# The later modulation vectors: from 64 small matmuls on TensorE to 24 products on VectorE

## The chip, the cores and the metric

The kernel runs on one core of one Trainium2 chip. The metric is the time of one execution on the device in microseconds (us), the median of several executions. Before the change it is 836.27 us (three runs, 836.22 to 836.33), so differences of half a microsecond can be read if a kernel like it is run a few times.

Names used below: TensorE (PE in the profile) multiplies matrices, VectorE (DVE) and ScalarE (ACT) do elementwise work, GpSimd (POOL) and SyncE (SP) mostly issue DMA here. HBM is the memory of the chip, SBUF the on-chip memory, of which the kernel uses 128 partitions.

## The reference

A transformer block on 2048 tokens of 1024 values, with six modulation vectors that come from one vector `c`:

```python
mod = (silu(c) @ w_mod).reshape(c.shape[0], 6, 1, -1)   # w_mod is 1024 x 6144
sa, ca, ga, sb, cb, gb = ...                            # six vectors of 1024
h = layernorm(x) * (1 + ca) + sa
x = x + ga * attention(h, wqkv, wo)     # linear attention: phi(q) (phi(k)^T v), 32 heads
h = layernorm(x) * (1 + cb) + sb
x = x + gb * (silu(h @ w_gate) * (h @ w_up)) @ w_down
```

All of it is in two-byte floats. `sa` and `ca` are needed at once. `ga`, `sb` and `cb` are the later vectors that the change is about: `ga` is needed as a row on all partitions (it multiplies the columns of `wo`), `sb` and `cb` as columns (one value per partition, for each of the 8 groups of 128 features).

## The kernel before

The tokens are handled in four chunks (`sc`). For each chunk TensorE makes the keys, the values and, before the next chunk's keys go on, the product of the last chunk's keys and values (`kv_phase`): 128 matmuls of 32x64. The later vectors are made between key groups:

```python
    def mod_rows(blks):                       # four 512-column blocks of w_mod at once
        ps = acc_b("modr")
        for j in range(DC):
            for g in range(4):
                mm(ps[32 * g:32 * g + 32, :], lhsT=sc32[:, j, :], rhs=blks[g][:, j, :],
                                 start=(j == 0), stop=(j == DC - 1))
        row = small.tile([P, NB], BF16, name="mrow", bufs=1)
        nc.scalar.copy(out=row[:], in_=ps[:])
        return row

    def mod_spread(k, row):                   # rows to HBM, and back as columns
        for g in range(4):
            nc.gpsimd.dma_start(out=mrow_dram[k, g:g + 1, :], in_=row[32 * g:32 * g + 1, :])
        cols = small.tile([P, 2 * DC], BF16, name="mcol", bufs=1)
        ...
            nc.gpsimd.dma_start(out=cols[:], in_=mrow_dram[1].rearrange("g (i p) -> p (g i)", p=P))
        nc.vector.tensor_copy(out=sbT[:], in_=cols[:, 0:DC])
        ...
    # ga_rows: the same for ga with 32 matmuls of 256 columns; its row goes to HBM
    # in four stores of 512 bytes and comes back on all partitions

    for sc in range(NSC):
        if sc > 0:
            k_phase(sc, 0, 2)
            kv_phase(sc - 1)
            k_phase(sc, 2, 4)
            if sc == 2:
                ga_rows(blks)
            if sc == 3:
                mod_spread(1, mod_rows(blks))
            k_phase(sc, 4, 8)
            ...
        v_phase(sc)
        ...
```

## Time and profile before

| | before |
|---|---|
| median time | 836.27 us |
| span of the profiled execution | 834.7 us |
| TensorE busy | 828.2 us, 99% |
| VectorE busy | 317.6 us, 38% |
| modulation matmuls of the later vectors | 0.99 + 1.84 us |

The page of the profile of before, part 1 (busy time of each engine, with the share of the span and the number of instructions), and the head of part 4 (the chain of work that ended last, by engine):

```profile
span 834.7 us, 11272 instructions
...
PE 828.2 (99%) x4641; PEld 378.6 (45%) x4641; DVE 317.6 (38%) x606; ACT 168.6 (20%) x253; POOL 67.5 (8%) x168
...
PE 95%; DMA 3%; SPq 1%; DVE 0%; issue 0%; ACT 0%
```

TensorE is busy for all but 6.5 us, and the chain is TensorE, save for loads in the start-up and 2.9 us of ScalarE and VectorE at 168.5 us. So a microsecond of TensorE work that is taken out anywhere after the start-up is a microsecond of time, as long as nothing makes TensorE wait in its place.

The chain of before around the two places (start, length, link of the chain, number of instructions):

```profile
95.55 0.99 PE modr L98 x32
...
120.82 1.15 PE kvp L98 x128
121.97 3.56 PE acc L98 x16
125.53 1.84 PE modr L98 x32
```

`modr` are the modulation matmuls; both are links, so 0.99 + 1.84 = 2.83 us is what their removal can bring.

### The profile page before, as it was taken

Reading aid. Unit: us, or ns where it says so; the run is one execution under the profiler, and the core shown is the slowest. Engines: PE = TensorE matmul, PEld = TensorE weight load, DVE = VectorE, ACT = ScalarE, POOL = GpSimd, SP = SyncE. Lnnn points to the kernel's source line nnn. Section 1 sums busy time; section 2 is a strip of 40 time slices with the busy share of each in tenths; the row PEclk is TensorE's granted clock in tenths of the full one; section 3 lists DMA queues with packets and bytes.
Section 4 is the critical chain, followed back from the end, with each engine's and each line's share of the span. In section 5 each row is a group of like instructions: output and inputs, shape, how many; then the busy total and the mean of one; then the engine's idle time right before and its main releaser. Section 6 shows DMA issues by size and latency. Waiting matters only on the chain.

```text
span 834.7 us, 11272 instructions
## 1 busy us (share of the span) xinstructions
PE 828.2 (99%) x4641; PEld 378.6 (45%) x4641; DVE 317.6 (38%) x606; ACT 168.6 (20%) x253; POOL 67.5 (8%) x168
## 2 busy tenths in 40 slices
PE   8999999999999999999999999999999999999998
PEld 3444444444444444444444444444444444444444
DVE  5755643587344335522222244211114431111122
ACT  3455443334211111101111110111110101111000
POOL 2101201111130201100000010000001100000000
PEclk9999999999999999999999999999999999999999
DMA  9873790129998644636434183662505529710011
GB/s 325 293 202 88 227 194 1 34 61 290 359 247 265 190 151 144 185 117 219 144 114 138 44 227 95 220 221 82 171 1 155 162 69 332 239 53 1 19 58 51
DMA packets 125748, 129.07 MB, mean 155 GB/s; under 512 B 34112, under 2 KB 106304, under 8 KB 125184
## 3 DMA queue, kind: packets, MB, share of 16 engines
q1 hardware_dynamic: 121440, 114.97, 45.7%
q0 software_dynamic: 3968, 12.99, 5.4%
q8 instruction: 36, 0.59, 0.3%
q10 hardware_dynamic: 288, 0.40, 0.1%
q14 instruction: 16, 0.13, 0.1%
HBM read 108.27 MB, written 12.72 MB: 145 GB/s over the span
## 4 chain that ended last, share of the span: by engine, by line
PE 95%; DMA 3%; SPq 1%; DVE 0%; issue 0%; ACT 0%
PE acc L98 88%; PE a_ps L98 7%; DMA wv<-in_A_wqkv_dram 1%; DMA x_sb<-in_A_x_dram 1%; DMA wme<-in_w_mod_dram 1%; PE kvp L98 1%; SPq L140 0%; PE modr L98 0%; PE den L98 0%; SPq L120 0%; DVE wo L577 0%; PE wf L98 0%; SPq L137 0%; DVE pq L292 0%; ACT eb L289 0%
## 5 line engine op out<-in xcount | busy, mean ns | idle before, releaser
L98 PE MATMUL acc<-h2T,wgu 128*128 128x512 bf16 x1792 | 387.6, 379 | 0.0
L98 PEld LDWEIGHTS <-wgu 128*128 128x128 bf16 x1792 | 175.3, 98 | 211.3
L98 PE MATMUL acc<-wd,gu 128*128 128x512 bf16 (+2 forms) x924 | 196.1, 373 | 0.0
L646 DVE TENSOR_TENSOR gu<-acc,e 128x512 bf16<-128x512 f32 x112 | 77.5, 692 | 289.9 <-PE acc L98 289.9
L645 ACT ACTIVATE e<-acc 128x512 f32<-128x512 f32 x112 | 66.9, 597 | 374.8 <-PE acc L98 374.8
L98 PEld LDWEIGHTS <-gu 128*128 128x128 bf16 x924 | 89.3, 98 | 104.5
L98 PEld LDWEIGHTS <-hT 128*128 128x128 bf16 x512 | 49.6, 98 | 60.0 <-issue 1.4
L667 DVE TENSOR_TENSOR e<-acc,gb_bc 128x512 f32<-128x512 f32 (+2 forms) x33 | 22.3, 675 | 131.5 <-PE acc L98 128.6
L98 PE MATMUL a_ps<-wo,pq 128*128 128x512 bf16 x256 | 57.4, 379 | 0.0
L98 PE MATMUL acc<-wk,hT 128*128 128x512 bf16 x256 | 57.1, 379 | 0.0
L98 PE MATMUL acc<-hT,wq 128*128 128x512 bf16 x256 | 56.8, 379 | 0.0
L98 PE MATMUL acc<-wv,hT 128*128 128x512 bf16 x256 | 56.1, 379 | 0.3 <-DMA wv<-in_A_wqkv_dram 0.3
L289 ACT ACTIVATE eb<-acc 128x512 bf16<-128x512 f32 x64 | 37.8, 596 | 74.1 <-PE acc L98 71.0
L228 ACT ACTIVATE xn<-x,nmr,rstd 128x1024 bf16<-128x1024 f32 x16 | 19.8, 1240 | 126.2 <-POOL nmr L226 126.2
L614 POOL DMA_DIRECT2D x_scratch<-x x16 | 9.9, 616 | 377.3 <-DVE x L607 377.3
L98 PEld LDWEIGHTS <-pq 128*128 128x128 bf16 x256 | 25.1, 98 | 30.2
L98 PEld LDWEIGHTS <-wq 128*128 128x128 bf16 x256 | 24.6, 98 | 29.8 <-issue 0.9
L290 DVE TENSOR_SCALAR eb<-eb 128x512 bf16<-128x512 bf16 x64 | 18.5, 294 | 49.4 <-ACT eb L289 49.3
L607 DVE TENSOR_TENSOR x<-a_ps,x_sb 128x512 f32<-128x512 f32 x32 | 22.1, 691 | 7.8 <-PE a_ps L98 7.7
L212 POOL TENSOR_TENSOR rstd<-veps,neg_half 128x1 f32<-128x1 f32 x32 | 17.9, 560 | 80.9 <-DVE veps L210 70.8
L327 ACT CAST v<-acc 128x512 bf16<-128x512 f32 x32 | 18.2, 582 | 23.2 <-PE acc L98 23.2
L670 DVE TENSOR_TENSOR ob<-e,x1r 128x512 bf16<-128x512 f32 (+2 forms) x33 | 22.3, 676 | 1.0
(82 smaller groups left out, 274.6 us busy)
## 6 DMA issues: line engine op xcount, KB each, us to landing
wgu<-in_B_w_gate_dram SPq DMA_DIRECT2D x28, 1024.0 KB, 7.3
wgu<-in_B_w_up_dram SPq DMA_DIRECT2D x28, 1024.0 KB, 8.8
x_sb<-in_A_x_dram SPq DMA_DIRECT2D x32, 256.0 KB, 7.2
x_scratch<-x POOLq DMA_DIRECT2D x16, 512.0 KB, 3.1
x1r<-x_scratch SPq DMA_DIRECT2D x31, 256.0 KB, 2.8
wd<-in_B_w_down_dram SPq DMA_DIRECT2D x7, 1024.0 KB, 7.3
wml<-in_w_mod_dram SPq DMA_DIRECT2D x6, 1024.0 KB, 9.0
rbc<-rden_scratch POOLq DMA_DIRECT2D x16, 256.0 KB, 9.3
```

The lines of the kernel that those rows point to most:

```text
L98: return tc.keep_in_program_order(nc.tensor.matmul(out, lhsT=lhsT, rhs=rhs, start=start, stop=stop))
L212: nc.gpsimd.tensor_tensor(out=rstd[:, 0:n], in0=veps[:, 0:n], in1=neg_half[:].to_broadcast([P, n]), op=ALU.pow)
L228: nc.scalar.activation(out=dst, in_=src, func=ACT.Identity, bias=nmr[:], scale=rstd[:, 0:1])
L289: nc.scalar.activation(out=e[:], in_=acc, func=ACT.Exp)
L290: nc.vector.tensor_scalar(out=e[:], in0=e[:], scalar1=1.0, scalar2=PHI_EPS, op0=ALU.min, op1=ALU.add)
L327: nc.scalar.copy(out=v[:, t * D + nb * NB:t * D + (nb + 1) * NB], in_=acc[:])
L607: nc.vector.tensor_tensor(out=x1[:, ns], in0=a_ps[:], in1=x_t[:, ns], op=ALU.add)
L614: nc.gpsimd.dma_start(out=x1_dram[st * P:(st + 1) * P, :], in_=x1[:])
L645: nc.scalar.activation(out=sg[:], in_=ps[0][:], func=ACT.Silu)
L646: gm = nc.vector.tensor_tensor(out=guT[sc][f // GPT][:, f % GPT, :], in0=ps[1][:], in1=sg[:], op=ALU.mult)
L667: nc.vector.tensor_tensor(out=yt, in0=y_ps, in1=gb_bc[:, ns], op=ALU.mult)
L670: nc.vector.tensor_tensor(out=ob, in0=yt, in1=x1r, op=ALU.add)
```

## The change

The intent is to take the later vectors off TensorE. Blocks of `w_mod` are read by transposing loads, so that output features lie on partitions and inputs along the free axis. VectorE multiplies each 128x1024 block by silu(c), held as a row on all partitions, and sums along the row; the sum is one column of `ga`, `sb` or `cb`. There are 24 such products, set between VectorE's other work. `sb` and `cb` are wanted as columns, so their way through HBM goes away. `ga` is wanted as a row, so its column now has to be turned, by way of HBM. The loads of `wo` and its eight multiplications by `ga` move to the last chunk, and some orders of issue change; the cut below leaves that out.

```diff
-    def mod_rows(blks):
-        ps = acc_b("modr")
-        for j in range(DC):
-            for g in range(4):
-                mm(ps[32 * g:32 * g + 32, :], lhsT=sc32[:, j, :], rhs=blks[g][:, j, :],
-                                 start=(j == 0), stop=(j == DC - 1))
 ... (ga_rows, mod_load, mod_spread go as well)
+    def mod_load(q, cols):
+        for h in range(2):
+            t = big("wmt", [DC // 2, D])
+            lo = q * D + h * NB
+            last = nc.sync.dma_start_transpose(t[:], w_mod[:, lo:lo + NB])
+            mod_steps.extend((t[:, i, :], cols[:, 4 * h + i:4 * h + i + 1]) for i in range(DC // 2))
+        return last
+
+    def mod_step(n, anchor=None):
 ...
+                last = nc.vector.scalar_tensor_tensor(out=rows, in0=rows, scalar=scale, in1=sc_row[:], op0=ALU.mult,
+                                               op1=ALU.mult, accum_out=col)
+
+    def ga_spread():
+        col = small.tile([P, DC], BF16, name="gcol", bufs=1)
+        nc.vector.tensor_copy(out=col[:], in_=gaT[:])
+        with nc.allow_non_contiguous_dma(reason="1024 elements, once"):
+            nc.gpsimd.dma_start(out=ga_dram[0].rearrange("(i p) -> p i", p=P), in_=col[:])
+        nc.gpsimd.dma_start(out=ga_bc, in_=ga_dram[:].to_broadcast([P, D]))
 ... (start-up: sc_row is made by 8 small matmuls in place of some warming matmuls)
             kv_phase(sc - 1)
-            k_phase(sc, 2, 4)
-            if sc == 2:
-                ga_rows(blks)
-            if sc == 3:
-                mod_spread(1, mod_rows(blks))
-            k_phase(sc, 4, 8)
 ...
+            k_phase(sc, 2, 8)
 ...
+        if sc + 1 < NSC:
+            with tc.issue_after(last_load[0].ins):
+                last_load[0] = mod_load(*((2, gaT), (3, sbT), (4, cbT))[sc])
```

More of the change, by code (lines that the diff above doesn't have):

```diff
@@ L116 @@
     x_tiles = {}
+    last_load = [None]
     def load_x(st, eng):
         x_sb = k2.tile([P, D], BF16, name="x_sb")
-        eng.dma_start(out=x_sb[:], in_=x2[st * P:(st + 1) * P, :])
+        last_load[0] = eng.dma_start(out=x_sb[:], in_=x2[st * P:(st + 1) * P, :])
         x_tiles[st] = x_sb
@@ L187 @@
     sbT = const.tile([P, DC], F32, name="sbT")
+    cbT = const.tile([P, DC], F32, name="cbT")
     cb1T = const.tile([P, DC], F32, name="cb1T")
+    gaT = const.tile([P, DC], F32, name="gaT")
+    sc_row = const.tile([P, D], BF16, name="sc_row")
     ga_t = ep.tile([P, NB], F32, name="e")
@@ L206, in build_masks @@
                 nc.gpsimd.memset(zmask[rs, hg, HG * h + hg:HG * h + hg + 1], 1.0)
+    last_veps, last_nmr = [None], [None]
     def rstd_of(mv, n):
         veps = small.tile([P, STC], F32, name="veps")
-        nc.vector.tensor_scalar_add(out=veps[:, 0:n], in0=mv[:, 0:n, 1], scalar1=LN_EPS)
+        last_veps[0] = nc.vector.tensor_scalar_add(out=veps[:, 0:n], in0=mv[:, 0:n, 1], scalar1=LN_EPS)
         rstd = small.tile([P, STC], F32, name="rstd")
@@ L225, in normalise_act @@
         nmr = small.tile([P, 1], F32, name="nmr")
-        nc.gpsimd.tensor_scalar(out=nmr[:], in0=mv[:, 0, 0:1], scalar1=rstd[:, 0:1], scalar2=-1.0,
+        last_nmr[0] = nc.gpsimd.tensor_scalar(out=nmr[:], in0=mv[:, 0, 0:1], scalar1=rstd[:, 0:1], scalar2=-1.0,
                                 op0=ALU.mult, op1=ALU.mult)
@@ L255, in ln1_norm @@
         if sc > 0:
-            nc.sync.dma_start_transpose(hTs[sc][:, :, t * P:(t + 1) * P], xn[:])
+            last_load[0] = nc.sync.dma_start_transpose(hTs[sc][:, :, t * P:(t + 1) * P], xn[:])
         return xn
@@ L314, in k_phase @@
             k_evac(sc, [g], accs)
+            mod_step(int(k_groups.index(g) in K_STEPS[sc]))
     def v_phase(sc):
@@ L327, in v_phase, with q_phase @@
                 nc.scalar.copy(out=v[:, t * D + nb * NB:t * D + (nb + 1) * NB], in_=acc[:])
-    def q_phase(sc, lo=0, hi=DC):
+    def q_phase(sc, lo=0, hi=DC, steps=0):
         if lo == 0:
@@ L337, in q_phase @@
             phi_to(pqs[sc][:, qc, :], acc[:])
+            mod_step(steps)
     def v_ones(v, lo):
@@ L353, in kv_phase @@
         else:
-            nc.vector.tensor_tensor(out=kv_acc, in0=kv_acc, in1=kvv, op=ALU.add)
+            with tc.issue_after(last_phi[0].ins):
+                nc.vector.tensor_tensor(out=kv_acc, in0=kv_acc, in1=kvv, op=ALU.add)
     def gb_load():
@@ L368, in gb_sum @@
                 nc.vector.scalar_tensor_tensor(out=gb_acc[:], in0=t[:], scalar=sc, in1=gb_acc[:], op0=ALU.mult, op1=ALU.add)
-    def ga_rows(blks):
-        ps = acc_b("modr")
-        H2 = NB // 2
-        for j in range(DC):
-            for g in range(4):
-                mm(ps[32 * g:32 * g + 32, 0:H2], lhsT=sc32[:, j, :], rhs=blks[g // 2][:, j, (g % 2) * H2:(g % 2 + 1) * H2],
-                   start=(j == 0), stop=(j == DC - 1))
-        row = small.tile([P, NB], BF16, name="mrow", bufs=1)
-        nc.scalar.copy(out=row[:, 0:H2], in_=ps[:, 0:H2])
-        for g in range(4):
-            nc.gpsimd.dma_start(out=mrow_dram[0, g:g + 1, 0:H2], in_=row[32 * g:32 * g + 1, 0:H2])
-        nc.gpsimd.dma_start(out=ga_bc.rearrange("p (g n) -> p g n", g=4),
-                            in_=mrow_dram[0, :, 0:H2].unsqueeze(0).to_broadcast([P, 4, H2]))
@@ L384 @@
-    gb_rows = []
-    def mod_load(cols):
-        blks = []
-        for lo in cols:
-            t = big("wml", [DC, NB])
-            nc.sync.dma_start(out=t[:], in_=wm_v[:, :, lo:lo + NB])
-            blks.append(t)
-        return blks
-    def mod_rows(blks):
-        ps = acc_b("modr")
-        for j in range(DC):
-            for g in range(4):
-                mm(ps[32 * g:32 * g + 32, :], lhsT=sc32[:, j, :], rhs=blks[g][:, j, :],
-                                 start=(j == 0), stop=(j == DC - 1))
-        row = small.tile([P, NB], BF16, name="mrow", bufs=1)
-        nc.scalar.copy(out=row[:], in_=ps[:])
-        return row
@@ L404 @@
-    mrow_dram = dram.tile([2, 4, NB], BF16, name="mrow_scratch")
-    def mod_spread(k, row):
-        for g in range(4):
-            nc.gpsimd.dma_start(out=mrow_dram[k, g:g + 1, :], in_=row[32 * g:32 * g + 1, :])
-        cols = small.tile([P, 2 * DC], BF16, name="mcol", bufs=1)
-        with nc.allow_non_contiguous_dma(reason="2048 elements, once"):
-            nc.gpsimd.dma_start(out=cols[:], in_=mrow_dram[1].rearrange("g (i p) -> p (g i)", p=P))
-        nc.vector.tensor_copy(out=sbT[:], in_=cols[:, 0:DC])
-        nc.vector.tensor_scalar_add(out=cb1T[:], in0=cols[:, DC:2 * DC], scalar1=1.0)
+    gb_rows = []
@@ new lines @@
+    ga_dram = dram.tile([1, D], BF16, name="ga_scratch")
+    mod_steps = []
+    def mod_load(q, cols):
[6 more added lines that the diff above has]
+    def mod_step(n, anchor=None):
+        if n == 0:
+            return
+        scale = 1.0
+        if anchor:
+            one = small.tile([P, 1], F32, name="one", bufs=1)
+            with tc.issue_after(last_nmr[0].ins):
+                nc.gpsimd.memset(one[:], 1.0)
+            scale = one[:]
+        with tc.issue_after(anchor or last_phi[0].ins):
+            for _ in range(n):
+                rows, col = mod_steps.pop(0)
+                last = nc.vector.scalar_tensor_tensor(out=rows, in0=rows, scalar=scale, in1=sc_row[:], op0=ALU.mult,
+                                               op1=ALU.mult, accum_out=col)
+        return last
@@ L415, in modulate_all @@
+    K_STEPS = [(), (), (0, 2), (0, 2, 4, 5, 6)]
+    V_STEPS = [0, 4, 4, 7]
+    def ga_spread():
[4 more added lines that the diff above has]
+        nc.gpsimd.dma_start(out=ga_bc, in_=ga_dram[:].to_broadcast([P, D]))
     def modulate_all(hT, scaleT, biasT):
@@ L459, in keep_warm, with keep_warm_f32 @@
             mm(acc[:], lhsT=sel[:, 0, :], rhs=sel[:], start=True, stop=True)
+    def keep_warm_f32(acc, n):
+        zeros = sel[:].rearrange("p h n -> p (h n)").bitcast(F32)
+        for _ in range(n):
+            mm(acc[:, 0:zeros.shape[1]], lhsT=zeros[:, 0:P], rhs=zeros, start=True, stop=True)
     gs = k_groups[0:6]
@@ L463 @@
     spare = accs[5]
-    keep_warm(spare, 9)
+    keep_warm_f32(spare, 4)
+    keep_warm(spare, 1)
     hT = hTs[0] = big("hT", [DC, SCW])
@@ L477 @@
         xns = [ln1_norm(*st0)] + [ln1_norm(*ln1_stats(0, t)) for t in range(1, 3)]
-        keep_warm(spare, 6)
+        keep_warm_f32(spare, 3)
         mod_rows_a(0)
         pe_transpose_tile(hT, xns[0], 0)
-        keep_warm(spare, 3)
+        for h in range(2):
+            for j in range(DC // 2):
+                mm(accs[h][:, j * P:(j + 1) * P], lhsT=scT[:, 4 * h + j:4 * h + j + 1].to_broadcast([P, P]), rhs=ident[:],
+                   start=True, stop=True)
+            nc.scalar.copy(out=sc_row[:, h * NB:(h + 1) * NB], in_=accs[h][:])
         mod_rows_a(1)
@@ L521 @@
             kv_phase(sc - 1)
-            k_phase(sc, 2, 4)
-            if sc == 2:
-                ga_rows(blks)
-            if sc == 3:
-                mod_spread(1, mod_rows(blks))
-            k_phase(sc, 4, 8)
-            if sc == 1:
-                blks = mod_load([2 * D, 2 * D + NB])
-            if sc == 2:
-                blks = mod_load([3 * D, 3 * D + NB, 4 * D, 4 * D + NB])
+            if sc == NSC - 1:
+                wo = [big("wo", [4, D]) for _ in range(2)]
+                for h in range(2):
+                    for g in range(4):
+                        with tc.issue_after(last_load[0].ins):
+                            nc.sync.dma_start(out=wo[h][g * DH:(g + 1) * DH, :, :], in_=wo_v[h, g])
+            k_phase(sc, 2, 8)
         v_phase(sc)
@@ L537 @@
             q_phase(0, 0, 6)
+        steps = mod_step(V_STEPS[sc], last_veps[0].ins if sc + 1 < NSC else None)
+        if sc == NSC - 1:
+            with tc.issue_after(steps.ins):
+                for cc in range(DC):
+                    w = wo[cc // 4][:, cc % 4, :]
+                    nc.vector.tensor_tensor(out=w, in0=w, in1=ga_bc, op=ALU.mult)
+        if sc == 2:
+            with tc.issue_after(last_veps[0].ins):
+                ga_spread()
         if sc + 1 < NSC:
@@ L545 @@
                 load_x(st, nc.sync)
-        if sc == 2:
-            wo = [big("wo", [4, D]) for _ in range(2)]
-            for h in range(2):
-                for g in range(4):
-                    nc.sync.dma_start(out=wo[h][g * DH:(g + 1) * DH, :, :], in_=wo_v[h, g])
-            for cc in range(DC):
-                w = wo[cc // 4][:, cc % 4, :]
-                nc.vector.tensor_tensor(out=w, in0=w, in1=ga_bc, op=ALU.mult)
-    q_phase(1, 0, 2)
+        if sc + 1 < NSC:
+            with tc.issue_after(last_load[0].ins):
+                last_load[0] = mod_load(*((2, gaT), (3, sbT), (4, cbT))[sc])
+    q_phase(1, 0, 1, 2)
+    q_phase(1, 1, 2)
     kv_phase(NSC - 1)
@@ L682 @@
     q_phase(2, 6, 8)
+    nc.vector.tensor_scalar_add(out=cb1T[:], in0=cbT[:], scalar1=1.0)
     q_phase(3, 0, 5)
```

## The prediction

> # Prediction
>
> **What bounds the kernel now.** TensorE. The page gives it 828.2 us busy of a span of 834.7 us (99%) at full granted clock, and the chain of waits is 95% TensorE. After the start-up (it ends at 31.5 us with a load of the V weights) the waits view shows one TensorE wait, 0.2 us. VectorE is busy 317.6 us (38%), but nearly full in places: from 97.2 to 106.3 us its timeline idles 0.3 us.
>
> **What the change removes.** The late vectors (ga, sb, cb) cost 64 small matmuls: 0.99 us at 95.5 us and 1.84 us at 125.5 us, both links of the chain of waits, so all 2.83 us are critical. Off the path go two ScalarE evictions (0.37, 0.59 us), eight row stores, a column load, and a 2.23 us VectorE wait for it.
>
> **What it adds.** VectorE gets 24 products of 128x1024, each summed along the row. The nearest operation in the trace (scalar-tensor-tensor, 128x1024, gb sum) takes 1.28 us. Bf16 tensor-tensors of that size go at 0.62 us (four in 2.50)[...]; with reading out the sum I estimate a pitch of 1.2 to 1.3 us, 30 us in all. In the start-up, 8 small matmuls and two ScalarE copies replace three warming matmuls, where TensorE waits for loads: neutral. Six 1 MB loads become transposing loads. A 256 KB transpose takes 1.23 us of queue and lands in 3.5 us; I estimate 5 us of queue and 8 to 15 us to land. Each pair has 23 us or more before its first use: no wait.
>
> **Does VectorE delay TensorE?**
> - First stretch (from 78 us): VectorE idles 6.5 us there; four products fit, and TensorE needs the result only near 87 us.
> - Second (from 107 us): four products end near 112.5 us; TensorE needs the activations at 116 us.
> - Third, the tight place: between 127 and 153 us VectorE must do 12 products, the eight wo multiplies (4.9 us, moved here) and six activation pairs of 0.95 us, before the bf16 kv state that TensorE transposes near 153.4 us (156.2 now, less 2.8). My sum ends at 138.2 us + 12 pitches: 152.6 us for 1.2, 153.9 for 1.3, 155.1 for 1.4. So a stall of 0 to 2 us, most likely 0 to 0.5.
>
> After 175 us nothing changes but the start.
>
> **Predicted time: 833.7 us** (2.8 saved, about 0.3 given back), range 832.9 to 836.0. Chances: faster by over 2% 0.01, within 2% 0.98, slower by over 2% 0.01.
>
> **What would show each step right or wrong.**
> - TensorE busy falls by about 2.8 us; no modulation matmuls in the chain after the start-up.
> - The products show 1.2 to 1.3 us each; VectorE busy rises by about 30 us.[...]
> - The only new TensorE wait is at the transpose of the kv state, for VectorE, under 2 us.
> - The transposing loads land within 15 us; no product waits for one.
> - The start-up ends within 0.3 us of before.
>
> **What would make it wrong.** A transposing load out of HBM much slower than one out of SBUF (above 23 us for a pair), which would block VectorE and the evictions; a pitch of 1.5 us, which would eat the gain in the third stretch; fp32 warming matmuls that fail to hold the clock; loads that delay the transposes of the next activations.

With reading out the sum it came to the pitch of 1.2 to 1.3 us that stands in the text, which is 30 us for 24 products; the forecast's own sum, 138.2 us + 12 pitches, is built on it. The nearest operation in the trace of before, at 1.28 us, lies in the same range. As for the fear at the end that the clock might not hold: the granted clock in the start-up (0 to 32 us) was 1.00 in before, and 1.00 in after.

## More of the kernel before

Note for later how the vectors reach HBM before: TensorE makes them as rows, and each store writes 512 or 1024 bytes in one run.

The line that turns out to matter is the first DMA in `ga_spread`. `"(i p) -> p i"` lets partition p write value i to place 128 i + p of a row of 1024: by this pattern no value lies beside another of its partition, so the store is 1024 pieces of two bytes, and pieces of 32 partitions lie in each 64 bytes of HBM. Such a piece is called a write in what follows; the traces do not count them (the profile of e4 has 57 packets for this store).

`kvp` is the product of keys and values: 128 matmuls in 1.15 us.

## The result, and the profile after

| | before | after |
|---|---|---|
| median time | 836.3 us (836.22 to 836.33, 4 runs) | 847.62 us (846.95 to 849.78, 4 runs) |
| ratio after / before | | 1.014 (95% interval 1.0121 to 1.0159) |
| TensorE busy | 828.2 us | 824.4 us |
| VectorE busy | 317.6 us | 344.8 us |

Ratios here and below are the mean time of one kernel's fast runs over the mean of the other's in the same rounds, so they are not quite the ratio of the medians quoted. The change costs 11.3 us where 2.6 us of gain were predicted. It stays within 2%, but the time lies well outside the predicted range of 832.9 to 836.0.

The page after, the same lines:

```profile
span 846.2 us, 11100 instructions
...
PE 824.4 (97%) x4503; PEld 380.6 (45%) x4582; DVE 344.8 (41%) x654; ACT 168.7 (20%) x253; POOL 63.0 (7%) x162
...
PE 97%; issue 2%; DVE 1%; ACT 0%; POOL 0%
```

TensorE's work did shrink, but the chain now has 2% of "issue", time in which TensorE waited for nothing that the profile can name. The waits view of after (in total, times, longest) says where:

```profile
PE kvp L98 <- issue: 9.4, 4, 6.8
PE acc L98 <- issue: 2.2, 7, 1.0
```

Before has no such line. The wait for VectorE that the prediction looked for, at the transposes of the kv state, isn't there. The chain of after shows the place, the product of the third chunk's keys and values and the key groups behind it:

```profile
119.48 0.80 PE kvp L98 x86
120.28 0.49 issue
120.77 0.19 PE kvp L98
120.96 0.12 issue
121.08 0.27 PE kvp L98 x5
121.36 1.73 issue
123.08 0.21 PE kvp L98 x2
123.29 6.79 issue
130.09 0.38 PE kvp L98 x12
130.46 0.35 issue
130.81 0.52 PE kvp L98 x22
131.33 0.33 issue
131.66 1.91 PE acc L98 x4
133.57 1.05 issue
134.62 11.70 PE acc L98 x45
```

The product that took 1.15 us in before runs 86 matmuls at full speed and then trickles until 131.33 us. Four matmuls of the next key group follow, then one more stop. What was going on beside it? The windows view of after (busy us of each engine with instructions, then the granted TensorE clock, the DMA share, and GB/s moved):

```profile
115.00:117.00 2.00, 2.00 (x11) 0.93 (x10) 1.80 (x6) 0.59 (x1) 0.00 (x0) 1.00 1.25 276
119.00:121.00 2.00, 1.47 (x90) 0.77 (x87) 1.97 (x5) 0.60 (x1) 0.00 (x0) 1.00 1.94 35
125.00:127.00 2.00, 0.00 (x0) 0.00 (x0) 0.00 (x0) 0.00 (x0) 0.00 (x0) 0.50 1.87 18
131.00:133.00 2.00, 1.67 (x26) 0.75 (x19) 0.43 (x1) 0.00 (x0) 0.73 (x2) 0.50 1.54 174
```

From 119 to 131 us the DMA engines hold transfers all the time (the share, 1.50 to 2.16, is that of transfers in progress) and move 15 to 35 GB/s, against 276 before and 174 after. And TensorE, which stands still from 123.29 us, is granted half its clock (0.50) from about 125 us, so that it also works at half speed when it goes on: four matmuls take 1.91 us at 131.66, and 1.03 us in e1 below.

Two DMA issues frame the stretch. The timelines of GpSimd and of SyncE in after (start, length, queue, what is issued, how many; in brackets the idle time before):

```profile
113.30 1.13 POOL L415 DMA_DIRECT2D ga_scratch<-gcol  x1 [5.34 <-DVE gcol L413]
131.45 0.59 POOL L416 DMA_DIRECT2D e<-ga_scratch  x1 [17.02 <-PE kvp L98]
110.97 20.68 SPq L388 DMA_TRANSPOSE wmt<-in_w_mod_dram  x2
```

The dense store of the `ga` column is issued at 113.30, and the load that reads it back only at 131.45 (the profile of after names TensorE's product as what released it; in e2 and e3 below it names the landing of the store). The last pair of transposing loads is issued at 110.97, the second one blocks the queue of SyncE until 131.65. So there are two suspects, the store and the transposing loads, and both are new.

### The profile page after: what moved, and what is told of

Same layout as the page of the kernel before. It is cut to its first block, busy times and chain, and to the rows that moved or that the text cites. A ratio compares the mean times of both kernels' runs of the same rounds, so it can differ in the third digit from the quotient of the medians.

```text
span 846.2 us, 11100 instructions
## 1 busy us (share of the span) xinstructions
PE 824.4 (97%) x4503; PEld 380.6 (45%) x4582; DVE 344.8 (41%) x654; ACT 168.7 (20%) x253; POOL 63.0 (7%) x162
## 4 chain that ended last, share of the span: by engine, by line
PE 97%; issue 2%; DVE 1%; ACT 0%; POOL 0%
PE acc L98 89%; PE a_ps L98 6%; PE kvp L98 1%; DVE stats L224 0%; PE mod_ps L98 0%; PE den L98 0%; ACT xn L234 0%; DVE wo L592 0%; PE tp L101 0%; PE wf L98 0%; DVE pq L298 0%; ACT eb L295 0%; POOL rstd L218 0%; DVE mv L225 0%; DVE veps L216 0%
## 5 line engine op out<-in xcount | busy, mean ns | idle before, releaser
L98 PE MATMUL acc<-wk,hT 128*128 128x512 bf16 x251 | 59.0, 392 | 1.7 <-issue 1.5
L234 ACT ACTIVATE xn<-x,nmr,rstd 128x1024 bf16<-128x1024 f32 x16 | 19.8, 1240 | 126.0 <-POOL nmr L232 126.0
L623 DVE BATCH_NORM_STATS2 stats<-x 128x6 f32<-128x512 f32 x32 | 22.2, 694 | 1.1
```

The lines of the kernel that those rows point to most:

```text
L98: return tc.keep_in_program_order(nc.tensor.matmul(out, lhsT=lhsT, rhs=rhs, start=start, stop=stop))
L234: nc.scalar.activation(out=dst, in_=src, func=ACT.Identity, bias=nmr[:], scale=rstd[:, 0:1])
L623: nc.vector.bn_stats(out=stats[:, nb, :], in_=x1[:, ns])
```

## The experiments

### The theories

- **Store**: the dense store of 1024 two-byte values is slow in itself, holds the DMA engines and through them TensorE.
- **Transposing loads**: the last pair of transposing loads out of HBM holds the engines, and the store only waits behind it.

In the expectations of e1 to e4 these are theories A and C; theory B there is that the store does harm only beside the transposing loads. Later expectations use the letters anew, each time with its meaning.

All kernels below give right results within the tolerance, the first two only because the error that they make is small. Where a kernel was looked at once, its time has no interval, and the record gives its state as unknown, where it calls all the repeated runs fast; such runs are used for differences of several microseconds and for their traces.

### e1: the same store, but each partition writes its 8 values in one run (wrong: the row is permuted)

```diff
-            nc.gpsimd.dma_start(out=ga_dram[0].rearrange("(i p) -> p i", p=P), in_=col[:])
+            nc.gpsimd.dma_start(out=ga_dram[0].rearrange("(p i) -> p i", i=DC), in_=col[:])
```

> One edit to the changed kernel: the store of the ga vector to HBM writes each partition's 8 values (16 bytes) side by side instead of 1024 single values of 2 bytes; same bytes, same place, WRONG RESULT ON PURPOSE (ga comes back in another order). Theory A (the 1024 two-byte writes block the DMA engines' write path, and TensorE's next block of instructions waits behind it): the stop of TensorE in the kv product at 120 us goes, the last pair of transposing loads lands in about 7 us each, time 832.5 to 834.5. Theory B (the two-byte store is harmful only beside transposing loads): the same here. Theory C (transposing loads and instruction fetch collide, whatever the store): stays at 845 to 849.

Measured: 835.25 us (834.82 to 836.12), before 836.39; ratio 0.9985 (0.9968 to 1.0001). The chain of e1 at the same place:

```profile
120.39 1.16 PE kvp L98 x128
121.54 0.16 issue
121.70 1.03 PE acc L98 x4
122.73 1.82 issue
124.55 9.89 PE acc L98 x45
```

The stop in the product is gone, with the transposing loads unchanged. The time lies 0.75 us above theory A's range. Set against the chain of after this also splits the loss. From the start of the product to the end of the 45 matmuls after takes 134.62 + 11.70 - 119.48 = 26.84 us, e1 14.05 us. Of the 12.8 us between them, "issue" makes up 8.9 (10.86 against 1.98), and the same matmuls running slower, at half clock, 3.9 (15.98 against 12.07). One stop stays, of 1.82 us, after the 4th matmul of the key group; it comes back below.

### e2: the last pair as plain loads (wrong: `cb` is then not `cb`)

```diff
+            if q == 4:
+                last = nc.sync.dma_start(out=..., in_=wm_v[:, :, lo:lo + NB])
+            else:
                 last = nc.sync.dma_start_transpose(t[:], w_mod[:, lo:lo + NB])
```

> One edit to the changed kernel: the last pair of loads (for cb) is an ordinary load of the same bytes into the same tiles instead of a transposing one, WRONG RESULT ON PURPOSE; the two-byte store stays. Theory A: the store still needs more than 10 us to land, and TensorE still stops for several us in the kv product: 840 or more. Theory B: the store lands within about 5 us, no stop, 833 to 835. Theory C: no stop, 833 to 835.

Measured, one look: 848.96 us. TensorE stops in the same product (7.7 us of "issue" in all) and after the 4th matmul behind it (3.4 us). The transposing pair is not needed for the harm.

### e3: the dense store twice, to two places

> One edit to the changed kernel: the two-byte store is made twice, to two places in HBM. Theories A and B: the time in which the engines crawl (14 us, from 117 to 131 us) doubles to some 28 us and the stop of TensorE grows by 10 to 14 us: 857 to 863. Theory C: no change, 846 to 850. Result correct.

Measured, one look: 854.48 us, 6.9 us more than after. The stop in the product is 10.6 us at its longest, the one behind it 5.1 us. All the expected times were missed (857 to 863, 846 to 850). A second store adds about half of what the first one does; I put that down to two stores that are partly under way together, which no run separates.

### e4, e9, e10, e11: the store alone, in a quiet stretch of the kernel before

The kernel before, with one more store out of an existing column at about 136 us, while TensorE makes values and no other transfer runs. Nothing reads it. Four forms, the number and spread of the writes being what differs:

```diff
+ga_dram2 = dram.tile([1, D], BF16)          # e4: 1024 two-byte writes, dense
+nc.gpsimd.dma_start(out=ga_dram2[0].rearrange("(i p) -> p i", p=P), in_=cols[:, 0:DC])
 # e9: the same with half the values, 512 writes
 # e10: D * 32 values of room, each value 64 bytes from the next:
+nc.gpsimd.dma_start(out=ga_dram2[0].rearrange("(i p w) -> p i w", p=P, w=32)[:, :, 0:1], in_=cols[:, 0:DC].unsqueeze(2))
 # e11: as e1, 128 runs of 16 bytes:
+nc.gpsimd.dma_start(out=ga_dram2[0].rearrange("(p i) -> p i", i=DC), in_=cols[:, 0:DC])
```

> The kernel before with one addition: the same two-byte store of 1024 values, from the column tile at about 136 us, when its DMA engines are idle (nothing reads what it writes; result correct). Theory A: the store takes 12 to 16 us from issue to landing all by itself, while the time stays within 1 us of before, as little else is in flight. Theory B: it lands in 2 to 5 us alone. Theory C: says nothing of the landing; time as before.

> The kernel before with a two-byte store of 512 values in the quiet stretch instead of 1024 (which took 13.3 us to land). If the number of writes sets the time[...]: 7 to 8.5 us. If the time is a fixed one of this store: 12 us or more. Kernel time as before. Result correct.

> The kernel before with the two-byte store of 1024 values in the quiet stretch, but each value goes to a place of its own, 64 bytes from the next, so that no two writes touch the same 64 bytes. If writes into the same few bytes wait for each other: it lands in under 6 us. If each small write costs the same wherever it goes: 12 to 15 us. Result correct.

> The kernel before with the same 1024 values stored in the quiet stretch as 128 runs of 16 bytes. If the number of writes sets the time: about 2 to 4 us to land. If the 2 KB into one place in HBM are slow by themselves: over 10 us. Result correct.

Measured: 836.05, 836.21, 836.27 and 836.13 us, so none of them costs time there. The DMA view of each, in this order (what is stored, how, KB, us from issue to landing):

```profile
ga_scratch<-mcol POOLq DMA_DIRECT2D x1, 2.0 KB, 13.3
```
```profile
ga_scratch<-mcol POOLq DMA_DIRECT2D x1, 1.0 KB, 13.9
```
```profile
ga_scratch<-mcol POOLq DMA_DIRECT2D x1, 2.0 KB, 2.9
```
```profile
ga_scratch<-mcol POOLq DMA_DIRECT2D x1, 2.0 KB, 1.7
```

Two kilobytes take 13.3 us to land with nothing else on the DMA engines. Half as many writes take as long, 13.9 us (the expectation of 7 to 8.5 us missed; half of 13.3 is 6.7), and the same 1024 two-byte writes spread over 64 KB take 2.9. So neither the amount nor the number of writes sets the time, nor that they are two bytes long. What fits all four runs is how many of them fall into the same small place: 32 per 64 bytes in e4 and in e9, four in e11, one in e10. Dividing gives an estimate of 13.3 / 32 = 0.4 us for each write into the same 64 bytes, if 64 bytes, the step of e10, is the size of the place, which no run tested.

Not every small write is dear: 128 runs of 16 bytes landed in 1.7 us (e11).

That e4 costs nothing shows something else: a slow store is not yet a stopped TensorE. This is taken up at e12.

### e5 and e6: the change without the dense store

e5 turns the column into a row by 8 small matmuls against the identity and has no store at all. e6 keeps the way through HBM but lets VectorE transpose 32x32 blocks first, so that runs of 64 bytes are stored:

```diff
 # e6
-            nc.gpsimd.dma_start(out=ga_dram[0].rearrange("(i p) -> p i", p=P), in_=col[:])
+        nc.vector.transpose(out=row, in_=col[:])          # 32x32 blocks
+        gv = ga_dram[0].rearrange("(i q r) -> q i r", q=HPC, r=DH)
+        for q in range(HPC):
+            nc.gpsimd.dma_start(out=gv[q], in_=row[q * DH:q * DH + DC, :])
```

> The changed kernel without the store to HBM and without the load back: ga is turned into a broadcast row by 8 small matmuls (0.45 us of TensorE by the cost of such matmuls in the start-up) in the last key phase. If the two-byte store is the whole of the loss: 833.5 + 0.45 = 833.9, range 833.3 to 834.6. If, as the contiguous-store run hints, about 1.8 us more are lost because TensorE's next block of instructions also queues behind the last pair of transposing loads: 835.3 to 836.2, with a gap of 1 to 2 us in TensorE near 122 us.

> The changed kernel with ga turned on VectorE (32x32 blocks) first, so that the store makes 32 writes of 64 bytes instead of 1024 of 2; result correct. If the number of writes sets the store's time: it lands in under 5 us, no long stop, the same time as the contiguous store, 834.5 to 836. If the time comes of anything else in the store (its size of 2 KB, its target in HBM, its queue): still above 845.

Measured in the same rounds, before 836.37: e5 834.89 us (ratio 0.998, 0.9967 to 0.9993), e6 834.92 us (0.9979, 0.9965 to 0.9993). Two quite different ways of doing without the dense store come to the same time, 12.7 us under after. e5 falls between its two expected ranges, e6 into its own. e6's four stores landed in 2.8 to 5.9 us, 3.2 in the median. TensorE's timeline of e6 at the place:

```profile
119.62 1.35 PE L98 MATMUL kvp<-v,pk 128*32 128x64 bf16 x128
121.13 1.02 PE L98 MATMUL acc<-wk,hT 128*128 128x512 bf16 x4 [0.16 <-issue]
123.34 6.87 PE L98 MATMUL acc<-wk,hT 128*128 128x512 bf16 x31 [1.18 <-issue]
```

The product runs through, and one stop is left, again after the 4th matmul. It cost 1.2 us of the predicted gain in this execution (0.87 in e5). It does not cost the same each time: e6's five runs reach from 833.88 to 835.68 us.

### e7 and e8: the last transposing pair earlier

The DMA table of the page of before has lines for instructions. This is the one that fits TensorE (packets, MB, share of the engines):

```profile
q8 instruction: 36, 0.59, 0.3%
```

That is 16 KB for each packet, and one packet for 258 of TensorE's 9282 instructions (4641 weight loads and as many multiplications). Between the first packet, at 17.7 us, and the last, at 817.2, there are 254 for each. That these packets are TensorE's I infer from this steady rate, since no view names the engine. I call what one packet brings a block of instructions, about 255. In before such a packet comes at 113.2 and at 122.6 us. In after there is none between 95.0 and 132.1 us. In all runs with a stop after the 4th matmul, e1, e2, e3, e5, e6 and after, it lies at the same place of the program, after 1976 instructions. (Counted here and below as twice the weight loads: some matmuls are missing from the traces, 4503 against 4582 loads in after.) My theory: that stop is a wait for a block that queues behind the last transposing pair, issued at 111 us. The packets support it. In five of the six runs TensorE goes on 2.2 to 2.6 us after the start of the late packet (after: 132.1 and 134.62; e6: 120.8 and 123.34). In the sixth, e2, the packet itself took 6.4 us, from 127.5, and TensorE went on at 134.99; e2 has no transposing pair there but the dense store, so it is not behind transposing loads alone that a block can be late. In e7 (e5 with this) and e8 (e6 with this) the last pair is issued right after the middle one:

```diff
-                last_load[0] = mod_load(*((2, gaT), (3, sbT), (4, cbT))[sc])
+                for a in (((2, gaT),), ((3, sbT), (4, cbT)), ())[sc]:
+                    last_load[0] = mod_load(*a)
```

> The run with ga by matmul, with one more edit: the last pair of transposing loads is issued right after the middle pair, some 20 us earlier, into a time in which the queue is idle. If the remaining gap of TensorE near 122 us comes from its instruction block queueing behind that pair: the gap goes and the time is 833.5 to 834.4, 1.5 to 2 us below the ga-by-matmul run. If it comes from anything else: equal to that run within 0.5 us.

> Both mends without any work on TensorE: the store in runs of 64 bytes and the last pair of transposing loads issued 20 us earlier. If the two causes (the 1024 writes, the instruction block behind the transposing loads) are all that was lost against the prediction: 833.0 to 834.0, the 2.8 us of the removed matmuls gained in full.

Measured in the rounds of e5 and e6: e7 833.87 us (ratio 0.9969, 0.9956 to 0.9981), e8 833.13 us (833.0 to 834.05; ratio 0.9963, 0.9951 to 0.9976). e8 beats both the kernel before and the change. e7 is 1.0 us under e5, where 1.5 to 2 were expected. The packet that came at 120.3 and 120.8 us in e5 and e6 comes at 117.4 and 117.6 in e7 and e8. TensorE's timeline of e8:

```profile
119.62 1.22 PE L98 MATMUL kvp<-v,pk 128*32 128x64 bf16 x128
121.00 9.23 PE L98 MATMUL acc<-wk,hT 128*128 128x512 bf16 x42 [0.16 <-issue]
```

Both stops are gone. 836.37 - 2.83 = 833.54: with them gone the whole predicted gain is there.

### e13: the same kernel as e6, with the block borders moved

e7 and e8 moved a load and might have helped in another way. e13 leaves every transfer of e6 as it is and puts more, shorter warming matmuls in the start-up, so that the rest of the program comes later in TensorE's instruction stream (the product of the third chunk starts after 1796 instructions in place of 1712):

```diff
-            mm(acc[:, 0:zeros.shape[1]], lhsT=zeros[:, 0:P], rhs=zeros, start=True, stop=True)
+            for _ in range(8):
+                mm(acc[:, 0:P], lhsT=sel[:, 0, :], rhs=sel[:, 0, :], start=True, stop=True)
```

> The kernel that stores the ga column in runs of 64 bytes (834.92, with one gap of 1.2 us after the 4th matmul of the key group behind the kv product), with each of its 7 warming matmuls of four-byte values replaced by 8 short ones of two-byte values, and so with some 90 more instructions on TensorE at start-up and the same data everywhere.[...] Theory (the gap is the wait for the next block of instructions): the gap after the 4th matmul goes, or moves to another matmul some 45 matmuls earlier, and if it moves into a stretch that the DMA engines leave free the time is 833.3 to 834.1. Rival (the gap is set by the data of that key group or by the semaphore that it waits for): the gap stays at the 4th matmul of that group, and the time stays at 834.6 to 835.3.

Measured: 833.65 us (833.34 to 833.93; before 836.31, ratio 0.9966, 0.9953 to 0.998), and no stop after the 4th matmul:

```profile
121.19 10.31 PE L98 MATMUL acc<-wk,hT 128*128 128x512 bf16 x47 [0.16 <-issue]
```

Apart from the start-up, what moved is where the borders of instruction blocks fall; the last pair is issued 0.7 us later than in e6. One packet now comes at 108.1 us, before that pair. With the packet times above, this shows that the stop was a wait for a block of instructions.

### e12: the dense store alone, ahead of the last kv product of before

Does the dense store stop TensorE by itself? The kernel before, its store now issued at 147.13 us, 4 us ahead of the product of the last chunk, with nothing else on the DMA engines:

```diff
-                nc.scalar.copy(out=v[:, t * D + nb * NB:t * D + (nb + 1) * NB], in_=acc[:])
+                vc = nc.scalar.copy(out=v[:, t * D + nb * NB:t * D + (nb + 1) * NB], in_=acc[:])
+                if sc == NSC - 1 and (t, nb) == (STC - 1, 0):
+                    gcol = small.tile([P, DC], BF16, name="gcol", bufs=1)
+                    with tc.issue_after(vc.ins):
+                        nc.scalar.copy(out=gcol[:], in_=sbT[:])
+                    with nc.allow_non_contiguous_dma(reason="1024 elements, once"):
+                        nc.gpsimd.dma_start(out=ga_dram2[0].rearrange("(i p) -> p i", p=P), in_=gcol[:])
```

> The kernel before, with nothing added but one dense store of 1024 two-byte values out of a column, issued by GpSimd some 4 us ahead of the last kv product (151.6 us in before), so that it is on its way while the 128 matmuls of that product run. No other DMA traffic of the core is made there: no transposing load, no load back. Theory A (the store alone holds TensorE up in the kv product, whatever else is on the DMA engines): idle time of some 4 to 11 us put down to 'issue' shows inside or straight after this kv product, and the time grows to 841 to 847. Theory B (TensorE stops for want of its next block of instructions, which queues behind the traffic of the DMA engines): the block that landed at 153.2 us in before lands late by as much as the store holds the engines, and the stop falls where that block starts to be needed, not necessarily in the kv product; with the engines otherwise empty this is at most a few us, 836 to 841. If the time is 836 to 837 with no stop, the store needs the transposing load next to it to do harm. In each case its own landing should be 13 to 14 us, as in the quiet stretch.

Measured, one look: 846.65 us, 10.3 us over before. TensorE's timeline of e12:

```profile
151.23 2.11 PE L98 MATMUL kvp<-v,pk 128*32 128x64 bf16 x126
160.63 0.49 PE L98 MATMUL kvp<-v,pk 128*32 128x64 bf16 x2 [7.29 <-issue]
```

Nearly the whole loss of the change (10.3 of 11.3 us) is made by one store of 2 KB, added to a kernel that has nothing else new but a 0.20 us copy on ScalarE. TensorE goes on 13.5 us after the store's issue, about when such a store lands (13.3 us in e4), and at half clock (0.50 in the windows view from 155 to 163 us). Theory B had allowed at most a few microseconds; theory A's range holds. This settles the first question: the store alone does it. It leaves the second, why here and not in the quiet stretch of e4.

### e14, e15, e16: what TensorE is held by

e14 is e12 with 29 more warming matmuls (58 instructions), to move the block borders against the product. e15 is e4 with 128 matmuls on constants, of the product's shape, put into the quiet stretch.

```diff
 # e14 (and e15): two matmuls of half the width for each warming matmul
-            mm(acc[:], lhsT=sel[:, 0, :], rhs=sel[:], start=True, stop=True)
+            for h in range(2):
+                mm(acc[:, 2 * h * P:(2 * h + 2) * P], lhsT=sel[:, 0, :], rhs=sel[:, 2 * h:2 * h + 2, :], start=True, stop=True)
 # e15, in the value product
+                    burst = acc_b("modr")
+                    for _ in range(128):
+                        mm(burst[0:DH, 0:2 * DH], lhsT=sel[:, 0, 0:DH], rhs=sel[:, 0, 0:2 * DH], start=True, stop=True)
 # e16: e12 with four matmuls of a quarter of the width for each warming matmul
```

> The kernel before with the dense store ahead of its last kv product (846.65, TensorE held 7.3 us after the 126th of the 128 small matmuls), with 29 more warming matmuls at start-up (each halved in width)[...]. Theory C (while such a store is outstanding, TensorE can go on for some 200 to 270 instructions, whichever they are, and is then held until the store is through): the stop stays at the 120th to 128th matmul of the kv product, ends some 13 us after the issue of the store, and the time is 845 to 848. Rival B (the stop is a wait for a block of instructions): the stop comes some 29 matmuls earlier, at about the 97th, or goes away.

> The kernel with the dense store in the quiet stretch (836.05, landing 13.3 us, TensorE not stopped; some 120 TensorE instructions ran in that time), with 128 matmuls of the kv product's shape (32x64) on constants, whose result nothing reads, put into the value product after its third group, some 2 us after the store's packets; and the 29 extra warming matmuls. Theory C (a store outstanding, and more than some 200 to 270 TensorE instructions in that time): TensorE is held at about the 90th to 128th of these matmuls until some 13 us after the store's issue, and the time is 844 to 849. Rival D (it is something of the kv product itself, its data or its accumulators): no stop, 837 to 838, which is 1.2 us for the matmuls added. Rival B (a block of instructions): a stop at about the 76th of them, where such a border lies.

> The same kernel, before with the dense store ahead of its last kv product, with 87 more warming matmuls (each cut into four), which is 174 TensorE instructions, so that the same place in the instruction stream (the 2597th instruction or so, where the long stop began in both runs so far, after the 126th and the 98th matmul) now falls after the 39th or 40th matmul of the kv product. Rival B (a fixed place in the stream, a border of instruction blocks): the long stop begins after the 39th or 40th matmul. Theory C' (a burst of small matmuls fills something that the store keeps from draining; the first short pauses came after the 76th and the 74th matmul, in after the 87th, 88th and 103rd): no pause before the 70th matmul, the first short pauses between the 70th and the 106th, the long stop between the 85th and the 128th. Time 845 to 848 by both.

Measured, one look each: 847.21, 841.70 and 844.20 us. TensorE's timeline of e14, then that of e16:

```profile
151.44 1.32 PE L98 MATMUL kvp<-v,pk 128*32 128x64 bf16 x98
159.97 1.07 PE L98 MATMUL kvp<-v,pk 128*32 128x64 bf16 x30 [7.21 <-issue]
```
```profile
152.62 1.22 PE L98 MATMUL kvp<-v,pk 128*32 128x64 bf16 x128
157.45 0.46 PE L98 MATMUL den<-pq,Zden 128*32 128x128 bf16 x20
161.77 0.56 PE L98 MATMUL den<-pq,Zden 128*32 128x128 bf16 x12 [3.86 <-issue]
```

In e14 the long stop came after the 98th matmul in place of the 126th, 28 matmuls earlier, as theory B had it. In e16 no exact expectation held, and the time lies below the expected 845 to 848: the product ran through at full speed with the store outstanding, which takes theory C' away, and the stop came later, in the next small matmuls. Counted in the program, the long stop begins after 2594 instructions in e12, 2596 in e14 and 2848 in e16: the same place twice, and then 252 to 254 instructions further, which is one block of about 255 within the few instructions that the count is good for. So in these three runs the long stop keeps to the grid of instruction blocks, whatever the work there is. It is not the point of a block at which the other stop lies: from 1976 to 2594 are 618 instructions, 2.4 blocks.

e15 missed all three expectations. The added matmuls took 3.8 us, because each was 30 ns long, and TensorE was not stopped in them. ScalarE was, though, as its timeline in e15 shows:

```profile
139.89 0.59 ACT L327 CAST v<-acc 128x512 bf16<-128x512 f32 x1 [1.14 <-PE acc L98]
150.84 2.05 ACT L327 CAST v<-acc 128x512 bf16<-128x512 f32 x4 [10.36 <-PE acc L98]
```

Four evictions of values run back to back at 150.84 us. TensorE had ended the first of these groups near 145.4 us, but ScalarE got the word only 13.2 us after the store's issue (137.65), 5.4 us late. e16 has the same: the evictions due from about 155.6 us on run at 161.80, 13.3 us after the issue.

Set side by side, the six runs with the store in the kernel before show one pattern:

| run | store issued | packet of TensorE instructions in the 13.3 us after it | held | until |
|---|---|---|---|---|
| e4 | 136.13 | none (134.9, then 152.5) | nothing | |
| e9 | 136.31 | none (135.1, then 152.8) | nothing | |
| e12 | 147.13 | 155.1 | TensorE | 160.63 |
| e14 | 147.34 | 154.3 | TensorE | 159.97 |
| e15 | 137.65 | 144.8 | ScalarE, waiting for TensorE | 150.84 |
| e16 | 148.53 | 156.8 | ScalarE, then TensorE | 161.77 |

Something is held in exactly those runs in which TensorE fetches a block of instructions while the dense store is outstanding, and it is let go within a microsecond of the store's expected landing (expected from e4: the traces of e12, e14, e15 and e16 record no landing for it). Why a fetch on one queue should wait for a store on another, no run shows. One other transfer was late beside the store: in after, the first transposing load of the last pair landed 20.3 us after its issue, where the first two pairs took 6.3 to 7.5. It had been issued 2.3 us ahead of the store, though. And the table is a correlation over six runs, with two things in it that a plain wait for the block does not explain: TensorE is held in e12 from 153.34 us, ahead of the packet at 155.1, and in all four runs the hold outlasts the packet by 3.9 to 4.7 us. What exactly is held behind the fetch, and why it is TensorE's next instructions in two runs and its signals to ScalarE in two others, no run separates; nor why TensorE begins to pause ahead of the grid: in after at instructions 1884 to 1900, 76 to 92 ahead of the stop after 1976, and in e12 and e14 with short pauses (0.1 to 0.3 us) after the 76th and the 73rd matmul, whose start the shift of the borders by 29 matmuls did not move with it.

## Why the prediction was wrong, point by point

- **The gain (2.83 us): right.** The modulation matmuls are gone from the chain, and e8, which is the change without its two new costs, stands at 833.13 against a predicted 833.7.
- **VectorE's costs: right.** A product takes 1.21 to 1.29 us in the trace, at a pitch of 1.14 to 1.21 us back to back, and 0.08 us to read the sum. The predicted pitch was 1.2 to 1.3. VectorE's busy time rose by 27.2 us (predicted 30).
- **"So a stall of 0 to 2 us, most likely 0 to 0.5" at the kv transposes: no harm done.** There is no such wait in after, nor in e8: in both VectorE had the bf16 state ready 0.7 us before TensorE transposed it (at 166.99 and 167.70 us in after, at 152.41 and 153.13 in e8).
- **The transposing loads: right for two pairs of three.** They landed in 6.3 to 7.5 us, sooner than the predicted 8 to 15, and a pair took 8.4 and 10.2 us of SyncE's queue, where 5 us were predicted for one. The last pair took 19.8 us in after, but 7.6 in e6 beside a store of 64-byte runs and 8.6 in e1, so it was a victim. No product waited for a load.
- **The failed step: "What the change removes" and "What it adds".** The prediction counts "eight row stores, a column load" as removed, and lists among what is added products, small matmuls and transposing loads. It never lists the new store of the `ga` column, 1024 two-byte writes. It seems to have been taken for a DMA off the critical path like those that it replaced; the text gives no reason. Measured, it is the largest term of the sum: +12.7 us (847.62 against 834.92 in e6, and 834.89 in e5), and +10.3 us when added alone to the kernel before (e12).
- **"The only new TensorE wait is at the transpose of the kv state": wrong.** The new waits are for no data at all. One is the stop that the dense store makes (9.4 us of TensorE in the kv product of after). The other, mis-sized at zero, is the wait for a block of instructions behind the last transposing pair: 1.0 us (e5 to e7) to 1.8 us (e6 to e8), and 1.3 us by moving the block borders alone (e6 to e13). The prediction asked of each load when its data would be needed, and not what else would queue behind it.

The steps from e8 to after are then 1.8 us for the late pair (833.13 to 834.92) and 12.7 for the dense store (834.92 to 847.62). They close because they are differences of the same three runs. What checks them are runs that took no part: e13 gives 1.3 for the first, and e12, one look, 10.3 for the second.

## What to carry to other kernels

A column of one value per partition was dear to scatter to HBM value by value here: 13.3 us to land (e4), and 10.3 us of time beside a kv product (e12). Turned on the chip first by 32x32 transposes on VectorE and stored in runs of 64 bytes it took 3.2 us to land (e6, median), and with 8 small matmuls against the identity it needed no store (e5); the two came to the same time, 834.92 and 834.89 us. Try these first where a change has such a store. Look over every DMA that a change adds, however few bytes it moves, and ask what else is in flight beside it, the instructions of the engines included. If the profile puts TensorE's idle time down to "issue" and to no engine, look for the packets of instructions in the DMA record and for a transfer that lands late, and move the suspect by itself into the old kernel: one such run settles more than many readings.
